# Products of zeros on TensorE in the planned gaps of a fused attention and MoE kernel, with a place for each in PSUM, and new planner constants

## The chip, the cores and the metric

One core of a Trainium2 chip runs the whole program. The metric is the device time of one execution in microseconds (us); of a kernel timed several times the median counts. TensorE (PE) multiplies, VectorE (DVE), ScalarE (ACT) and GpSimd (POOL) do the elementwise work, and the DMAs are issued from the queue of SyncE (SP), or early on from that of ACT. TensorE writes its results to PSUM, which has 8 banks of 512 float32 columns. TensorE's clock has two levels, 1.2 and 2.4 GHz; the profile shows which of them was granted as a share of the upper one (0.5 or 1.0, or something between for a stretch that holds both).

## The reference

Three stages follow one another, on 4 batches of 576 tokens:

```python
scores = scale * q @ k.T                       # 4 x 8 heads, 576 x 576, head size 64
scores = scores + cum[:, None] - cum[None, :]  # cum: running sum of log f
attn = softmax(causal(scores)) @ v             # (4, 8, 576, 64) -> x: (2304, 512)
y = (x @ w_a) * (x @ w_b) @ w_out              # 512 -> 1536 -> 512
h = y @ w_in                                   # 512 -> 1024
out = layernorm(h * softmax(h)) * g_ln @ w_out2
```

All inputs and outputs are float32. Every large product is computed from operands split in a high and a low part, as three products added up in PSUM.

## The kernel before

The kernel doesn't issue its instructions in a fixed order. It first describes all work as operations (`op`, from line 78), each with an engine or a choice of engines, a planned duration, a key (its rank among the operations that are ready) and the buffers that it reads and writes. `Sched.run` (line 118) then plans a time line: on each engine it takes the ready operation that can start first, by rank among equals, books its planned duration, and gives buffers and PSUM banks to it. The result is a list sorted by planned start, and the instructions are issued in that order, so each engine's queue runs in the planned order, whatever the real times are. A product with n columns is planned at n/2400 us and a little (`t_mm`, line 44), which is the rate at the upper clock level. All ranks come from the constants in `Y` (line 291).

The work of the first part, up to some 470 us, is attention, head by head, with the first MoE products mixed in. The first batch's eight heads come twice: first their first 256 tokens (kind `K0`), then the rest (`K1`); the other 24 heads come whole (`KF`). One head goes through: a transpose of q and k on TensorE (line 842); the split of both by ACT (lines 862, 873), DVE (865, 877) and POOL (851); products that find the largest score of each row (906, with a mask added by 910) and their row maxima on DVE (930); a transpose of the maxima (948) and a copy of them by ACT (952); the scores (980, 984, 988); the exponential and its split by ACT (1031, 1047) and DVE (1053); the weighing of v (1088); and the division by the sum (1110 to 1142). As soon as 256 tokens of all heads of a batch are there, `up_unit` (line 1202) multiplies them with blocks of w_a and w_b (line 1211), whose weights were loaded and split by `load_cols` (lines 652 to 699). Attention's sums live in the banks from `state["lo"]` up; `lo` is 1 at first (line 491) and rises to 2 once the up products have begun, which use the banks below it (`bank_unit`, line 499); it would rise to 3 for a stream of tokens numbered `L3` or higher (line 1206), and the numbers go from 0 to 5. An up unit holds two banks at once, and while it has 256 tokens only the lower 256 columns of each are used. After about 610 us only the last two stages run.

At the end of the function stands a filler: a product of the identity, taken as bf16 (`identb`), with 256 columns of `cmask` that hold only zeros, written to the upper half of bank 0 (lines 1725 and 1726). It is meant for gaps of TensorE's plan: from the time `at` on, for every planned TensorE operation that starts before `F1`, a gap over `FG` is filled to the share `FF` of its length with fillers of 0.109 us each. The time from which gaps are counted is

```python
at, todo = max(CONST.last[x].done for x in ("ident", "cmask")) + 0.2, []
```

and `CONST.last["cmask"]` is the operation described last that writes `cmask`. The mask itself is set at the start (the operation that calls `k_cmask`, lines 531 and 532). The load of the layer norm's weights, which lie in the mask's memory, names it as written too (lines 1386 and 1387), with the rank of the end of attention:

```python
op(("SP", 0.68), Z[-1], lat=2.0, fn=lambda: issue(
    out=gln, in_=moe2_g_ln.rearrange("(c p) -> p c", p=P)), w=[(CONST, "gln"), (CONST, "cmask")], nbytes=4e3)
```

Of the kernel before, what the change touches and what calls it, by code (L numbers as in the profile page):

```python
# [45 lines left out]


class Buf:
    __slots__ = ("cls", "slot", "left", "users", "last", "readers", "free", "cand", "pool", "lo", "skip", "at")

    def __init__(self, cls, cand=None, pool=None):
        self.cls, self.cand, self.pool = cls, cand, pool
        self.lo = 0
        self.skip = cls == "att"
        self.slot = None
        self.left = 0
        self.users = []
        self.last = {}
        self.readers = {}
        self.free = 0.0  # L60
        self.at = 0.0


class Op:
    __slots__ = ("n", "opts", "fn", "key", "deps", "after", "ready", "bufs", "done", "eng", "port", "lat", "nbytes", "start", "scheduled", "nwait", "dma", "lean")


class Sched:
# [21 lines left out]
    def op(self, opts, key, fn, r=(), w=(), after=(), lat=0.0, port=False, nbytes=0, lean="BIAS"):  # L90

        o = Op()
        o.n = len(self.ops)
        o.opts = [opts] if isinstance(opts, tuple) else list(opts)
        o.dma = o.opts[0][0] == "SP"
        o.lean = lean
        if o.dma and key < Y["D2"]:
            o.opts.append(("ACT", o.opts[0][1]))
        o.fn, o.key, o.lat, o.port, o.nbytes = fn, key, lat, port, nbytes
        deps = set(after)  # L100
        bufs = []
        for b, p in r:
            if p in b.last:
                deps.add(b.last[p])
            b.readers.setdefault(p, []).append(o)
            if b not in bufs:
                bufs.append(b)
        for b, p in w:
            if p in b.last:
                deps.add(b.last[p])  # L110
            for x in b.readers.get(p, ()):
                if x is not o:
                    deps.add(x)
            b.readers[p] = []
            b.last[p] = o
            if b not in bufs:
                bufs.append(b)
        deps.discard(o)
        for b in bufs:
            b.left += 1  # L120
            b.users.append(o)
        o.deps, o.bufs = deps, bufs
        o.after = []
        o.scheduled = False
        o.ready = 0.0
        self.ops.append(o)
        return o
# [163 lines left out]
Y = {  # L291
    "Z0": 13.6157,
    "T0": 4.814,
    "T1": 6.0827,
    "TA": 11.0028,
    "TF": 18.2246,
    "U0": 1.7014,
    "U1": 0.2661,
    "UF": 2.0658,
    "UL": 1.2999,  # L300
    "LEAD": (1.2959, 6.2184),
    "SHRINK": 1.9788,
    "W0": 39.7443,
    "WD0": 2.7456,
    "WN": 3,
    "WD1": 0.0,
    "WD2": 11.7263,
    "EZ": 8.5785,
    "EO": 17.1538,
    "TE": 28.5361,  # L310
    "DL": 0,
    "BIAS": 0.3046,
    "UO": (7.4065, 7.7687, 10.1476),
    "UD": 22.6745,
    "UK": 375.6785,
    "L3": 13,
    "TL": (0.0, 0.0),
    "F1": 262.9889,
    "FG": 0.1893,
    "FF": 0.7352,  # L320
    "RA": 1,
    "HM": 0,
    "HC": 2,
    "YC": 20.1189,
    "T2": 11.1014,
    "TB": 1,
    "HB": 1,
    "F2": 344.7825,
    "LATE": -0.6454,
# [28 lines left out]
def kernel(  # L358
# [14 lines left out]
    nc = tc.nc  # L373
    B, H, S, D = q.shape
    P = 128
    NP = H // 2
    BH = B * H
    NT, DM = out.shape
    KD = DM // P
    FF = moe_w_a.shape[1]  # L380
# [118 lines left out]
    def bank_unit(last, c):  # L499
        def cand(_):  # L500
            if last and c >= NF - Y["HB"]:
                return [(b, 1) for b in range(4, 8)]
            return [(b, 1) for b in range(8 if last else state["lo"])]
        return cand
# [10 lines left out]
    def k_set(s, part, eng=None):  # L515
        b = type("B", (), {"slot": s})
        if part < 2:
            cs = slice(0, 2 * P) if part == 0 else slice(2 * P, SP)
            eng.memset(SB(b).bitcast(F32)[D:, cs], -1.0)
            eng.memset(MB(b).bitcast(F32)[D:, cs], 0.0)  # L520
            eng.memset(MB(b).bitcast(F32)[D:D + 2, cs], 1.0)
            if part == 0:
                eng.memset(mts[:, s], 0.0)
                eng.memset(mts[:, s, 0:2], 1.0)
        else:
            nc.gpsimd.memset(SA(b).bitcast(F32)[:, S:SP], 0.0)
            nc.gpsimd.memset(SB(b).bitcast(F32)[:D, S:SP], 0.0)
            nc.gpsimd.memset(MB(b).bitcast(F32)[:D, S:SP], 0.0)
# [18 lines left out]
    for s in range(NSET):  # L547
        o = op([("POOL", 1.0), ("DVE", 1.0)], 20.0, None, w=[(CONST, f"pad{s}a")])
        o.fn = lambda s=s, o=o: k_set(s, 1, ENG[o.eng])
        op(("POOL", 0.6), 20.0, lambda s=s: k_set(s, 2), w=[(CONST, f"pad{s}")])  # L550
    PADS = [(CONST, "set0"), (CONST, "set1"), (CONST, "set2")]
    PADS2 = [(CONST, f"pad{s}{x}") for s in range(NSET) for x in ("", "a")]

# [647 lines left out]
    def up_unit(i, c, key, last):  # L1201
        b, q0, q1 = STR[i]
        n_ = q1 - q0
        u = [s_.buf("unit", bank_unit(last, c if i == NS - 1 else 0)) for _ in range(2)]
        u[0].lo = 3 if i >= Y["L3"] else 2
        uo = (0, n_) if len(u) == 1 else (0, 0)

        def mm(m, ks):
            for kk in ks:
                for n, (wp, xx) in enumerate(((0, 0), (1, 0), (0, 1))):  # L1210
                    nc.tensor.matmul(  # L1211
                        bank(u[m % len(u)], uo[m], n_), lhsT=wv(m, wp, c)[:, kk], rhs=xsv(i, xx, kk),
                        start=(kk == 0 and n == 0), stop=(kk == KD - 1 and n == 2))

        if c < Y["PK"] and i <= B:
            parts = [(m, (kk,)) for kk in range(KD) for m in range(2)]
        elif c == NF - 1 and i <= B:
            parts = [(m, (kk, kk + 1)) for kk in (0, 2) for m in range(2)]
        else:
            parts = [(m, range(KD)) for m in range(2)]  # L1220
        for j, (m, ks) in enumerate(parts):
            rx = [(xsb[i][p], (s, p)) for p in ks for s in "hl"]
            rw = [(WB[c], ((m, k_), s)) for k_ in ks for s in "hl"]
            op((PE, t_mm([n_] * 3 * len(ks))), key + Y["UK"] + 0.01 * j, lambda m=m, ks=ks: mm(m, ks),
               r=rx + rw, w=[(u[m % len(u)], m)])
        at = s_.buf("at")
        gt = s_.buf("gt")
        atv = lambda: ats[:, :n_]
        gtv = lambda: gts[:, gt.slot * XT:gt.slot * XT + n_]

        op(("ACT", t_act(n_, True)), key - 50.0, lambda: nc.scalar.copy(  # L1231
            out=atv(), in_=bank(u[0], 0, n_)), r=[(u[0], 0)], w=[(at, 0)])
        op(("DVE", t_dve(n_)), key - 50.0, lambda: nc.vector.tensor_tensor(  # L1233
            out=gtv(), in0=bank(u[-1], uo[1], n_), in1=atv(), op=ALU.mult),
           r=[(u[-1], 1), (at, 0)], w=[(gt, 0)])
        op(("SP", 0.44), key - 50.0, lat=1.45, fn=lambda: issue(out=gs[i][c], in_=gtv()),
           r=[(gt, 0)], w=[(GD, (i, c))], nbytes=512.0 * n_)
# [484 lines left out]
        fn(*a)  # L1722
    order = s_.run(state)

    def filler():
        nc.tensor.matmul(ps[:, 2 * P:512], lhsT=identb, rhs=cmask[:, :2 * P], start=True, stop=True)

    def fill(us):  # L1730
        return lambda: [filler() for _ in range(int(us / 0.109))]

    at, todo = max(CONST.last[x].done for x in ("ident", "cmask")) + 0.2, []
    for o in order:
        if o.eng == PE and o.start < Y["F1"]:
            gap = o.start - at
            if gap > Y["FG"]:
                todo.append((at, fill(gap * Y["FF"])))
            at = max(at, o.start + dict(o.opts)[PE])
    def emit(o):  # L1740
        now[:] = [o]
# [37 lines left out]
```

## Time and profile before

| | |
|---|---|
| median of 3 executions | 931.98 us (931.57 to 932.89) |
| the profiled execution | 932.68 us |
| its span, first to last instruction | 931.0 us |
| mean granted TensorE clock in the records | 0.983 |
| TensorE busy | 892.6 us, 96% of the span, 4926 products |
| DVE, ACT, POOL busy | 637.7, 474.9, 169.9 us (69, 51, 18%) |

Three ways of reading are used below. The windows view gives for any stretch the busy time of each engine and the granted clock. The list of a line's instructions gives the shortest, the median and the longest duration of each kind. The chain of waits follows the end of the program back to its start. A product's record in the timeline lasts longer than its turn on the engine, as the next one starts before it ends; the chain's pieces, or the distance of two starts, give the time that one takes from the engine.

### The profile page before, as it was taken

To read this page: it belongs to the slowest core of one execution; us is meant where nothing else is said; L and a number is where in the kernel's file an instruction comes from. 1 tells how busy PE (TensorE), PEld (TensorE's weight loads), DVE (VectorE), ACT (ScalarE), POOL (GpSimd) and SP (SyncE) were. 2 spreads that over 40 slices of the span, in tenths; PEclk is the share of its full clock that TensorE was granted. 3 is DMA by queue.
4 is the path that set the end of the run, shared out by engine and by line. 5 is a ranking of instruction groups with operands and counts; after the bars stand their busy time and mean duration, and the time that the engine had idled before them with its cause. 6 is when DMAs were issued, how large, how long until landed. Compare 5 with 4: busy or idle time off the path is not lost.

```text
span 931.0 us, 14134 instructions
## 1 busy us (share of the span) xinstructions
PE 892.6 (96%) x4926; PEld 775.5 (83%) x4926; DVE 637.7 (69%) x1238; ACT 474.9 (51%) x892; POOL 169.9 (18%) x297
## 2 busy tenths in 40 slices
PE   5878989999999999999999999999999999999996
PEld 3768978999888888888888898988888888888884
DVE  6768897777765457665476255789687777767784
ACT  3776785766664546555565143555333434243342
POOL 5556665232231103111111000000000000000000
PEclk9978998999999999999999999999999999999999
DMA  6244654433433323322266233353211111111101
GB/s 149 66 118 129 182 157 107 100 89 88 96 81 81 83 76 87 98 68 62 68 227 209 98 123 109 114 165 106 69 46 46 46 46 45 46 40 42 33 23 35
DMA packets 109947, 85.00 MB, mean 91 GB/s; under 512 B 69778, under 2 KB 91412, under 8 KB 109876
## 3 DMA queue, kind: packets, MB, share of 16 engines
q1 hardware_dynamic: 105508, 81.78, 30.9%
q10 hardware_dynamic: 4368, 2.32, 1.0%
q8 instruction: 39, 0.64, 0.3%
q14 instruction: 32, 0.26, 0.1%
HBM read 57.38 MB, written 19.55 MB: 83 GB/s over the span
## 4 chain that ended last, share of the span: by engine, by line
PE 91%; DVE 3%; ACT 3%; DMA 1%; issue 1%; POOL 0%; ACTq 0%; DVEq 0%; SPq 0%
PE ps L1211 31%; PE ps L1493 16%; PE ps L1686 11%; PE ps L1088 10%; PE ps L1579 9%; PE ps L988 3%; PE ps L906 3%; PE ps L980 3%; PE ps L842 2%; PE ps L1671 2%; DVE mts L930 1%; PE ps L948 1%; DMA nat<-in_q_dram 1%; PE ps L910 0%; DVE sets L865 0%
## 5 line engine op out<-in xcount | busy, mean ns | idle before, releaser
L1211 PE MATMUL ps<-xs,wt 128*128 128x256 f32 (+1 forms) x1728 | 331.7, 344 | 1.0 <-ACT xs L1178 0.3
L1211 PEld LDWEIGHTS ps<-xs,wt 128*128 128x128 f32 x1728 | 271.6, 193 | 34.4 <-POOL xs L1183 0.5
L1088 PE MATMUL ps<-pexp,VS 128*128 128x64 f32 (+5 forms) x600 | 104.6, 322 | 5.5 <-DVE sets L865 4.4
L1088 PEld LDWEIGHTS ps<-pexp,VS 128*128 128x128 f32 x600 | 96.5, 205 | 10.8 <-DVE sets L865 4.5
L1493 PE MATMUL ps<-wt,sets 128*128 128x512 f32 (+1 forms) x420 | 91.8, 370 | 0.0
L1493 PEld LDWEIGHTS ps<-wt,sets 128*128 128x128 f32 x420 | 72.9, 189 | 12.8
L1686 PE MATMUL ps<-wt 128*128 128x512 f32 x324 | 80.4, 393 | 1.8 <-DVE wt L1677 1.0
L1233 DVE TENSOR_TENSOR fw<-ps,fw 128x256 f32<-128x256 f32 (+1 forms) x72 | 40.0, 555 | 59.1 <-PE ps L1211 37.9
L1579 PE MATMUL ps<-wt,xs 128*128 128x512 f32 x306 | 79.3, 392 | 0.0
L1231 ACT COPY fw<-ps 128x256 f32<-128x256 f32 (+1 forms) x72 | 34.6, 481 | 79.5 <-PE ps L1211 70.3
L1053 DVE TENSOR_TENSOR pexp<-fw,pexp 128x768 fp32r<-128x768 f32 (+1 forms) x45 | 45.6, 1014 | 42.5 <-ACT pexp L1047 42.0
L1686 PEld LDWEIGHTS ps<-wt 128*128 128x128 f32 x324 | 59.9, 188 | 15.1 <-DVE wt L1677 1.9
L1481 ACT CAST wt<-nat 128x512 fp32r<-128x512 f32 (+1 forms) x60 | 34.6, 580 | 69.0 <-PE ps L1493 64.7
L1040 POOL TENSOR_SCALAR_AFFINE_SELECT fw<-fw 128x128 f32<-128x128 f32 (+1 forms) x120 | 36.4, 332 | 169.4 <-ACT fw L1031 169.3
L1579 PEld LDWEIGHTS ps<-wt,xs 128*128 128x128 f32 x306 | 56.5, 188 | 11.2
L933 DVE CUSTOM_DVE_ANT_0 ps<-ps,cmask 128x512 f32<-128x512 f32 (+4 forms) x100 | 53.8, 553 | 15.2 <-PE ps L906 12.9
L1485 DVE TENSOR_TENSOR wt<-nat,wt 128x512 fp32r<-128x512 f32 (+1 forms) x60 | 38.0, 635 | 28.6 <-ACT wt L1481 27.3
L980 PE MATMUL ps<-sets 128*128 128x320 f32 (+4 forms) x200 | 52.5, 310 | 2.8 <-ACT fw L1031 0.9
L988 PE MATMUL ps<-sets 67*128 67x288 f32 (+6 forms) x200 | 53.5, 342 | 0.2
L906 PE MATMUL ps<-sets 66*128 66x512 f32 (+2 forms) x192 | 48.5, 350 | 3.5 <-DVE sets L877 1.8
L1031 ACT ACTIVATE fw<-ps 128x768 f32<-128x768 f32 (+1 forms) x48 | 39.5, 836 | 23.2 <-PE ps L988 22.5
L1047 ACT CAST pexp<-fw 128x768 fp32r<-128x768 f32 (+1 forms) x48 | 41.2, 859 | 9.8 <-POOL fw L1040 9.4
(173 smaller groups left out, 1464.0 us busy)
## 6 DMA issues: line engine op xcount, KB each, us to landing
gs<-fw SPq DMA_DIRECT2D x36, 256.0 KB
nat<-gs SPq DMA_DIRECT2D x36, 256.0 KB
fw<-in_moe_w_out_dram SPq DMA_DIRECT2D x15, 512.0 KB
sets<-sets SPq DMA_DIRECT2D x48, 144.0 KB
fw<-in_moe_w_b_dram SPq DMA_DIRECT2D x10, 512.0 KB
fw<-in_moe_w_a_dram SPq DMA_DIRECT2D x9, 512.0 KB
nat<-gs SPq DMA_DIRECT2D x36, 128.0 KB
nat<-in_k_dram SPq DMA_DIRECT2D x33, 128.0 KB
```

Of the source, the lines that this page charges most:

```text
L906: nc.tensor.matmul(bank(ms[part], o, w), lhsT=MB(st)[:D + 2, i * P:(i + 1) * P], rhs=SB(st)[:D + 2, k0:k0 + w], start=True, stop=not pm)
L933: nc.vector.tensor_tensor_reduce(out=x, in0=x, in1=cmask[:n, off:off + w], scale=1.0, scalar=-3.0e38, op0=ALU.add, op1=ALU.max, accum_out= ...
L980: nc.tensor.matmul(dst, lhsT=SA(st)[:, ks], rhs=MA(st)[:, q0:q1], start=True, stop=False)
L988: nc.tensor.matmul(dst, lhsT=SB(st)[:depth, ks], rhs=MB(st)[:depth, q0:q1], start=False, stop=True)
L1047: op(("ACT", t_act(n, K.pm)), key + K.rk[5] + 6.8 + 0.9 * i, lambda bh=bh, n=n, pf=pf: nc.scalar.copy(out=pexp[:, 64 * bh.slot:64 * bh.slo ...
L1053: o.fn = lambda o=o, bh=bh, bl=bl, n=n, pf=pf: ENG[o.eng].tensor_tensor(out=pexp[:, 64 * bl.slot:64 * bl.slot + n], in0=pf(), in1=pexp[:, ...
L1088: nc.tensor.matmul(bank(u, K.uo + q0, q1 - q0), lhsT=V[:, vp], rhs=src[:, o:o + q1 - q0], start=(k_ in K.first and ip == 0), stop=(k_ in K ...
L1211: nc.tensor.matmul(bank(u[m % len(u)], uo[m], n_), lhsT=wv(m, wp, c)[:, kk], rhs=xsv(i, xx, kk), start=(kk == 0 and n == 0), stop=(kk == K ...
L1233: op(("DVE", t_dve(n_)), key - 50.0, lambda: nc.vector.tensor_tensor(out=gtv(), in0=bank(u[-1], uo[1], n_), in1=atv(), op=ALU.mult), r=[(u ...
L1493: nc.tensor.matmul(bank(py, 512 * d, n), lhsT=WO[c][0][:, wp * DM:(wp + 1) * DM][:, ds_], rhs=ghv(gb, gp)[:, :n], start=(c == 0 and i == 0 ...
L1579: nc.tensor.matmul(bank(bk, 0, 512), lhsT=yc(yx, yp)[:, kk], rhs=wi(wx, wp, kk), start=(n == 0), stop=(n == 5))
L1686: nc.tensor.matmul(bank(po, 0, DM), lhsT=zp[:, c], rhs=w2(c, wp), start=(c == 0 and i == 0), stop=(c == NF2 - 1 and i == 2))
```

## The change

The filler products get their own place. The operation that first writes the mask is kept in `MASKS`, where it is described, and `at` is taken from that. `place(at)` looks at the planned use of the banks at a gap's start: if an up unit of 256 tokens is in the middle of its sum (`half`), the filler goes to the spare upper half of that unit's bank and neither starts nor ends a sum; else it goes to the free bank whose next use is farthest off, with a start and an end of its own; if no bank is free, the gap stays. `FG` falls from 0.1893 to 0, `FF` goes from 0.7352 to 0.7329, `F1` from 262.99 to 268.18. Some forty other constants of `Y` change, most of them ranks, so the planned order changes.

```diff
     "T1": 6.0827,          ->  5.9693
     "U0": 1.7014,          ->  2.802
     "U1": 0.2661,          ->  1.3074
     "WD2": 11.7263,        ->  11.4893
     "UD": 22.6745,         ->  19.9599
     "F1": 262.9889,        ->  268.1794
     "FG": 0.1893,          ->  0.0
     "FF": 0.7352,          ->  0.7329
     "HB": 1,               ->  0
     "EL": -2.8131,         ->  2.403
...
+    MASKS = [CONST.last["ident"], CONST.last["cmask"]]
     PADS = [(CONST, "set0"), (CONST, "set1"), (CONST, "set2")]
...
         u = [s_.buf("unit", bank_unit(last, c if i == NS - 1 else 0)) for _ in range(2)]
+        for x in u:
+            x.half = len(u) == 2 and n_ == 2 * P
...
-    def filler():
-        nc.tensor.matmul(ps[:, 2 * P:512], lhsT=identb, rhs=cmask[:, :2 * P], start=True, stop=True)
-    def fill(us):
-        return lambda: [filler() for _ in range(int(us / 0.109))]
-    at, todo = max(CONST.last[x].done for x in ("ident", "cmask")) + 0.2, []
+    held = [(b, min(o.start for o in b.users), max(o.done for o in b.users),
+             [o.start for o in b.users if o.eng == PE])
+            for q in s_.queue.values() for b in q if b.pool == "bank" and b.users]
+    def place(at):
+        next_ = [1.0e9] * 8
+        for b, t0, t1, mm in held:
+            if b.half and min(mm) < at <= max(mm):
+                return b.slot, False
+            for x in range(b.slot, b.slot + b.free):
+                if t1 >= at:
+                    next_[x] = min(next_[x], 0.0 if t0 <= at else t0)
+        x = max(range(8), key=lambda x: next_[x])
+        return (x, True) if next_[x] > 0.0 else None
+    def fill(us, x, alone):
+        def go():
+            for _ in range(int(us / 0.109)):
+                nc.tensor.matmul(ps[:, 512 * x + 2 * P:512 * x + 512], lhsT=identb, rhs=cmask[:, :2 * P],
+                                 start=alone, stop=alone)
+        return go
+    at, todo = max(o.done for o in MASKS) + 0.2, []
     for o in order:
         if o.eng == PE and o.start < Y["F1"]:
             gap = o.start - at
-            if gap > Y["FG"]:
-                todo.append((at, fill(gap * Y["FF"])))
+            if gap > Y["FG"] and place(at):
+                todo.append((at, fill(gap * Y["FF"], *place(at))))
             at = max(at, o.start + dict(o.opts)[PE])
```

## Rows read from the trace of the kernel before

**Rows 1.** The page: TensorE's busy time, and the granted clock in 40 slices.

```profile
PE 892.6 (96%) x4926; PEld 775.5 (83%) x4926; DVE 637.7 (69%) x1238; ACT 474.9 (51%) x892; POOL 169.9 (18%) x297
...
PEclk9978998999999999999999999999999999999999
```

**Rows 2.** Windows: stretch; its length, PE, PEld, DVE, ACT, POOL busy; granted clock, DMA.

```profile
13.00:52.00 39.00, 33.71 (x153) 28.97 (x154) 24.73 (x55) 25.14 (x62) 21.50 (x33) 1.00 0.38 104
52.00:83.20 31.20, 21.87 (x117) 18.54 (x115) 24.42 (x35) 21.07 (x43) 17.70 (x17) 0.73 0.43 122
55.90:59.40 3.50, 2.92 (x14) 2.66 (x15) 3.50 (x6) 2.35 (x5) 0.95 (x1) 0.52 0.33 91
63.00:73.00 10.00, 7.33 (x32) 6.56 (x33) 7.68 (x11) 7.36 (x17) 6.53 (x6) 0.50 0.29 78
79.90:83.20 3.30, 3.30 (x17) 2.81 (x15) 2.26 (x4) 0.75 (x2) 2.63 (x3) 0.50 0.53 167
83.20:130.00 46.80, 46.39 (x370) 44.18 (x369) 40.32 (x61) 37.42 (x74) 28.39 (x27) 1.00 0.62 174
130.00:151.30 21.30, 15.93 (x86) 13.37 (x85) 15.75 (x28) 12.47 (x27) 13.18 (x20) 0.76 0.47 116
137.90:144.30 6.40, 5.86 (x26) 5.56 (x27) 3.76 (x7) 2.82 (x5) 4.42 (x7) 0.50 0.71 164
148.00:151.30 3.30, 3.30 (x16) 2.99 (x15) 2.03 (x4) 2.19 (x5) 0.70 (x2) 0.50 0.73 188
151.30:253.90 102.60, 100.88 (x754) 96.11 (x753) 77.95 (x155) 66.75 (x113) 31.76 (x65) 1.00 0.37 90
253.90:257.20 3.30, 3.30 (x14) 2.73 (x13) 2.17 (x3) 3.05 (x5) 1.86 (x4) 0.50 0.66 144
258.00:610.00 352.00, 352.00 (x1916) 307.44 (x1915) 204.00 (x381) 177.24 (x292) 43.89 (x99) 1.00 0.36 107
610.00:931.00 321.00, 313.15 (x1513) 261.06 (x1511) 237.42 (x499) 126.77 (x273) 1.56 (x2) 1.00 0.18 55
```

**Rows 3.** Weight loads of line 910 in four stretches: shortest, median, longest ns; starts.

```profile
L910 PEld LDWEIGHTS <-ident x16: 146/146/146, 13.7 to 49.8; 128*128 128x128 bf16 x16
...
L910 PEld LDWEIGHTS <-ident x5: 98/98/99, 52.7 to 54.7; 128*128 128x128 bf16 x5
...
L910 PEld LDWEIGHTS <-ident x1: 146/146/146, 81.3 to 81.3; 128*128 128x128 bf16 x1
...
L910 PEld LDWEIGHTS <-ident x8: 98/98/99, 92.3 to 116.7; 128*128 128x128 bf16 x8
```

**Rows 4.** The chain of waits: two runs of line 1211's 256-column products (start, us).

```profile
50.16 2.03 PE ps L1211 x9
...
89.32 2.96 PE ps L1211 x24
```

**Rows 5.** Groups of TensorE up to 270 us: the bf16 products at their widest.

```profile
L910 PE MATMUL ps<-cmask,ident 128*128 128x128 bf16 x48 | 12.7, 269 | 0.0
...
L984 PE MATMUL ps<-ident,cmask 128*128 128x128 bf16 x32 | 9.1, 284 | 0.0
```

**Rows 6.** Timelines of POOL and TensorE: the mask, and the first product of scores.

```profile
3.30 0.29 POOL L532 TENSOR_SCALAR_AFFINE_SELECT cmask<-cmask 128x128 bf16<-128x128 bf16 x1
...
13.38 0.55 PE L906 MATMUL ps<-sets 66*128 66x256 f32 x1 [0.43 <-issue]
```

**Rows 7.** The last products on TensorE, with the idle time before them.

```profile
910.36 1.10 PE L1671 MATMUL ps<-ident,xrw 128*128 128x128 f32 x8 [1.25 <-DVE xrw L1637]
...
925.76 0.39 PE L1686 MATMUL ps<-xs,wt 128*128 128x512 f32 x1
```

**Rows 8.** TensorE's waits up to 270 us: total us, times, longest.

```profile
PE ps L948 <- DVE mts L930: 8.9, 8, 1.9
...
PE ps L1211 <- ACT fw L1231: 0.2, 1, 0.2
```

More of the change, by code (lines that the diff above doesn't have):

```diff
@@ L48 @@
 class Buf:
-    __slots__ = ("cls", "slot", "left", "users", "last", "readers", "free", "cand", "pool", "lo", "skip", "at")
+    __slots__ = ("cls", "slot", "left", "users", "last", "readers", "free", "cand", "pool", "lo", "skip", "at", "half")
     def __init__(self, cls, cand=None, pool=None):
-        self.cls, self.cand, self.pool = cls, cand, pool
+        self.cls, self.cand, self.pool, self.half = cls, cand, pool, False
         self.lo = 0
@@ L293 @@
     "T0": 4.814,
-    "T1": 6.0827,
+    "T1": 5.9693,
     "TA": 11.0028,
     "TF": 18.2246,
[L297 to L302, printed above, removed]
+    "U0": 2.802,
+    "U1": 1.3074,
+    "UF": 2.0785,
+    "UL": 1.1356,
+    "LEAD": (1.2959, 6.0955),
+    "SHRINK": 1.795,
     "W0": 39.7443,
@@ L306 @@
     "WD1": 0.0,
-    "WD2": 11.7263,
+    "WD2": 11.4893,
     "EZ": 8.5785,
-    "EO": 17.1538,
+    "EO": 17.3183,
     "TE": 28.5361,
@@ L313 @@
     "UO": (7.4065, 7.7687, 10.1476),
-    "UD": 22.6745,
+    "UD": 19.9599,
     "UK": 375.6785,
-    "L3": 13,
+    "L3": 15,
     "TL": (0.0, 0.0),
-    "F1": 262.9889,
-    "FG": 0.1893,
-    "FF": 0.7352,
+    "F1": 268.1794,
+    "FG": 0.0,
+    "FF": 0.7329,
     "RA": 1,
@@ L323 @@
     "HC": 2,
-    "YC": 20.1189,
+    "YC": 21.644,
     "T2": 11.1014,
     "TB": 1,
-    "HB": 1,
+    "HB": 0,
     "F2": 344.7825,
     "LATE": -0.6454,
[1 row of a table removed]
[1 row of a table added]
     "BA": -0.177,
```

16 rows, old and new, of the table Y are left out of this document.

## The prediction

> **What bounds the kernel now.** I read the page first: TensorE is busy for 96% of the span, and its granted clock dips only in the first 260 us [rows 1]. The windows view, cut where the clock changes, then splits the kernel in two [rows 2]. From 151 us on TensorE is all but full: 1.7 us idle up to 253.9, none from 258 to 610, and 7.9 us after 610, of which 4.9 lie behind its last product (925.76 + 0.39 = 926.15, to 931.0) [rows 2, 7]. What comes earlier there ends the program earlier, and what TensorE does twice makes it later. Before 151 us it has slack: idle 5.3 us in stage A (13 to 52), 9.3 in stage B (52 to 83.2), 5.4 in stage C (130 to 151.3), and only 0.4 in the stretch between B and C.
>
> Six stretches stand at a granted clock of 0.50 to 0.52 (one of them, D, at 253.9): 3.5, 10.0, 3.3, 6.4, 3.3 and 3.3 us [rows 2]. The seventh is hidden. The records give stage A a clock of 1.00, but a weight load of line 910 takes 146 ns there 16 times of 16, from 13.7 to 49.8 us, just as at 81.3, where 0.50 is recorded, and 98 ns from 52.7 on and wherever else 1.00 is recorded [rows 2, 3]. So by the durations all of stage A ran at 1.2 GHz, with TensorE 86% busy. A 256-column product takes 2.03/9 = 0.226 us at the lower level and 2.96/24 = 0.123 at the upper [rows 4], so 45% of TensorE's time at the lower level would go. Busy time there: 33.71 in A, 2.92 + 7.33 + 3.30 = 13.55 in B, 5.86 + 3.30 = 9.16 in C, 3.30 in D; at 45%: 15.3, 6.2, 4.2 and 1.5, in all 27.2 us. That is the ceiling of what the clock alone can return.
>
> **The fillers.** The change adds them; it doesn't move them. The widest bf16 products in the first 270 us have 128 columns and belong to lines 910 and 984 [rows 5]; a filler has 256, and none is there. The code says why: the gaps were counted from the last writer of the mask, which is the load at the end of attention, beyond F1. Now they are counted from the real mask, ready at 3.59 us [rows 6].
>
> How much zero work is that? The planner books products at the upper clock, so its gaps are idle time plus what the lower clock costs. Busy from 13 to 258 is 222.9 us (33.71, 21.87, 46.39, 15.93, 100.88, 3.30, and 0.8 to 258, full) [rows 2], 196 at the upper clock. If that stretch falls from 245 to some 230 us, 34 us of gap stand there, and about 5 before 13 us. At 0.733, that is 29 us of zeros, some 265 fillers at the booked 0.109 us, 0.123 by the nearest row [rows 4], and a quarter of each gap stays as margin.
>
> **What the clock returns**, if the fillers hold it up. In a stage where TensorE has room, the next engine takes over, and I price it by the shares that DVE and ACT reach in the nearest stretch with a full clock and a full TensorE, 83.2 to 130: DVE 40.32/46.8 = 0.86, ACT 37.42/46.8 = 0.80 [rows 2].
> A: TensorE needs 33.71 - 15.3 = 18.4, DVE 24.73/0.86 = 28.8, ACT 25.14/0.80 = 31.4. ACT is late next: 39.0 becomes 31.4, so -7.6. Ends: 0 and -15.3.
> B: DVE 24.42/0.86 = 28.4, ACT 26.3; 31.2 becomes 28.4, so -2.8. Ends: 0 and -6.2.
> C: DVE 15.75/0.86 = 18.3; 21.3 becomes 18.3, so -3.0. Ends: 0 and -4.2.
> D: TensorE is full through and behind it, so all of it counts: -1.5.
> Together -14.9, all of it kept, since TensorE has no slack behind it.
>
> **What the fillers cost.** TensorE works in order, so a filler that is still running when its successor is ready delays it and all behind it. At the upper clock the quarter of margin covers that. At the lower it does not: 0.733 x 0.226/0.109 = 1.52 of the gap. This must happen until the clock first rises. Up to 13.38 us the first scores wait for the decay sums, not for TensorE [rows 6], which hides most of it. I take one more lapse of the shortest length seen, 3.3 us, at 0.52 each: +1.7. Ends: 0, and the 29 us if every filler stood in the way; the low end is nearer, as TensorE's idle in A, B and C (20 us) shows real gaps at real places.
>
> **The rest.** The new ranks reorder a TensorE that is full from 151 us on, so they can win there no more than its idle, 1.7 us, and the last pair's wait of 1.25 [rows 2, 7]; EL puts one pair's closing products elsewhere in just that tail. They could also lose as much. I take 0 between -3 and +3. HB lets the last up unit use any bank, where TensorE is full: 0, between the same ends. L3 rises from 13 to 15 and is compared with numbers up to 5: 0. The marks and `place` run before launch: 0.
>
> Sum: -14.9 + 1.7 = -13.2. The profiled execution took 932.68, so 919.5; the median stands 0.7 below it, so **918.8 us**.
>
> **A rule of the notes.** The Trainium skill, in "TensorE: Matmul & The Clock Gate", Part 1, says that the low clock is the resting state and that sustained activity releases it; by that alone a TensorE that is 86% busy for 39 us would not have stayed low. The rows disagree: 146 ns throughout. The same page warns in its caveats on clock events that the recorded ones have been seen to be unreliable, which fits the 1.00 beside 146 ns. By the first rule term A would go, and the sum would be that of rival 1.
>
> **The rivals.**
> 1. Stage A gains nothing: it was not slow by its clock, as the recorded 1.00 says, but by its waits. Then B, C and D give -7.3, less 1.7: -5.6, which is 926.4 by the median. For it: the record, and 5.3 us of idle. Against: 146 ns, and the clock was up at 52.7 us, right behind nine dense 256-column products that end at 52.2 [rows 3, 4]; a filler has as many columns. Chance 0.12.
> 2. The fillers wait. Each goes to a bank that is free by the plan; where the bank's last reader is late, TensorE stands still and all behind it too. The waits of line 948 for DVE cost 8.9/8 = 1.1 us each, that of line 1211 for its bank's reader 0.2 [rows 8]. Twelve waits of 1.1 eat the whole gain: 932. The Trainium skill's "PSUM — Partial Sum Buffer", section on bank collisions, asks for that order, since two engines must not touch one bank at a time; no run here shows it yet. Against: the bank with the farthest next use has often long been idle. Chance 0.05.
> 3. Nothing is emitted after all (no bank is found, or gaps are shorter than one filler), and only the ranks act: 932, within 3. Against: attention leaves bank 0 alone at first. Chance 0.03.
> 4. Slower: the clock stays low in stage A with the fillers in place. Its planned gap is 31.4 - 18.4 = 13.0 us, the zeros 9.5 booked and 9.5 x 0.226/0.109 = 19.7 real; TensorE then needs 33.7 + 19.7 = 53.4 where the stage took 39.0: +14.4, so some 946. It decides from the share of the stage that runs low: warm the sum is 18.4 + 9.5 = 27.9, cold 53.4, and 39.0 is reached at (39.0 - 27.9)/(53.4 - 27.9) = 44%. For it: 39 us at 86% busy did not raise the clock. Against, as in rival 1: dense products did. Chance 0.08.
>
> **The numbers.** The forecast case has 0.72. Its ends: -27.2 with the idle of A to C also shrinking (down to about 900), and a few us short of nothing. The range of 902 to 930 holds it but for 0.05, and rival 1; rivals 2 to 4 lie outside. No change means within 0.2%, 1.9 us, about what a measurement of this kernel can tell. Faster: 0.72 + 0.12 + a little of rivals 2 and 3, 0.86. Same: 0.05. Slower: 0.08 and 0.01 of rival 3, 0.09.
>
> **What would show it.** Right: some 265 bf16 products of 256 columns before 268 us; weight loads of line 910 at 98 ns from about 13 us on; the six low stretches gone; ACT and DVE at 0.80 or more in the first 50 us; line 1211's first full run before 80 us instead of 89; from there the same sequence, 13 us earlier, to the end. Wrong: 146 ns beside fillers (rival 4), waits of TensorE put down to a filler's bank (rival 2), or ACT and DVE no denser while TensorE idles between zeros (rival 1, or a chain of latencies that I priced too low).

## The result, and the profile after

The changed kernel takes 917.05 us (median of 4 executions, 916.50 to 921.45), the kernel before, run beside it, 932.43: a ratio of 0.9846, with a 95% interval of 0.9813 to 0.9878. The profiled execution took 916.50 us, its span 914.8, so 16.2 us less than the span of before; by the medians the gain is 15.4 us. The forecast was 918.8, its range 902 to 930.

The page of the kernel after, its lines of TensorE's busy time and of the granted clock in 40 slices:

```profile
PE 897.6 (98%) x5241; PEld 780.7 (85%) x5241; DVE 637.0 (70%) x1240; ACT 472.0 (52%) x886; POOL 170.3 (19%) x301
...
PEclk9999999999999999999999999999999999999999
```

There are 5241 - 4926 = 315 more products than in [rows 1], and no slice shows a low clock any more. What they are stands in the list of one line's instructions after; line 1747 is the new filler, line 911 the old line 910:

```profile
L1747 PEld LDWEIGHTS <-ident x315: 97/98/151, 1.4 to 255.5; 128*128 128x128 bf16 x158
L1747 PE MATMUL ps<-cmask,ident x315: 269/273/421, 3.3 to 255.5; 128*128 128x256 bf16 x158
...
L911 PEld LDWEIGHTS <-ident x21: 97/98/101, 13.6 to 45.8; 128*128 128x128 bf16 x21
```

All 315 are fillers, and line 911's weight loads take 97 to 101 ns from the first one at 13.6 us on, where [rows 3] had 146: by the durations the first stage now runs at 2.4 GHz. The windows of the kernel after, cut at the same work as [rows 2] where the order allows it (columns as there):

```profile
13.00:42.74 29.74, 28.05 (x243) 24.16 (x242) 25.60 (x53) 23.77 (x59) 19.41 (x29) 1.00 0.47 128
42.74:74.00 31.26, 28.82 (x233) 24.75 (x231) 27.16 (x41) 25.81 (x51) 22.40 (x25) 1.00 0.51 141
74.00:150.00 76.00, 74.47 (x604) 68.57 (x603) 63.65 (x109) 53.93 (x110) 45.86 (x55) 1.00 0.54 151
150.00:254.00 104.00, 103.83 (x755) 98.50 (x754) 74.06 (x148) 67.94 (x109) 31.56 (x65) 1.00 0.38 92
258.00:594.00 336.00, 336.00 (x1827) 293.26 (x1827) 195.07 (x361) 167.26 (x274) 38.90 (x94) 1.00 0.36 108
```

To see where the 16.2 us came from, two marks serve that stand in both orders: the eighth transpose of row maxima, which ends stage A, and the last up product. In the timelines, before and then after:

```profile
51.99 0.61 PE L948 MATMUL ps<-ident,mts 128*1 128x128 f32 x2
```

```profile
42.74 0.38 PE L949 MATMUL ps<-ident,mts 128*1 128x128 f32 x2
```

And in the list of the up products, first before, then after (the last number ahead of the forms is the last start):

```profile
L1211 PE MATMUL ps<-xs,wt x1728: 277/389/775, 43.6 to 605.8; 128*128 128x256 f32 x96, 128*128 128x512 f32 x96
```

```profile
L1214 PE MATMUL ps<-xs,wt x1728: 277/387/496, 36.3 to 589.5; 128*128 128x256 f32 x96, 128*128 128x512 f32 x96
```

Stage A gave 51.99 - 42.74 = 9.25 us. From there to the last up product it was 553.8 us and is 546.8: another 7.0. Behind that the same time passes: 931.0 - 605.8 = 325.2 before, 914.8 - 589.5 = 325.3 after. Among the waits of TensorE after (us in total, times, longest), up to 280 us:

```profile
PE ps L1747 <- POOL cmask L531: 3.3, 1, 3.3
PE ps L1089 <- DVE sets L866: 1.9, 1, 1.9
...
PE ps L949 <- DVE mts L931: 0.8, 3, 0.4
```

The waits for DVE's row maxima shrank from 8.9 us [rows 8] to 0.8: zeros stand in most of that time now. No filler waits for a reader of its bank: TensorE's only wait at line 1747 is that for the mask; the fillers' weight loads wait 1.4 us for the identity, and 2.3 us in three gaps for which the profile names no releaser.

### The profile page after: what moved, and what is told of

The parts are those of the page before. It is cut to its first block, busy times and chain, and to the rows that moved or that the text cites. A ratio compares the mean times of both kernels' runs of the same rounds, so it can differ in the third digit from the quotient of the medians.

```text
span 914.8 us, 14766 instructions
## 1 busy us (share of the span) xinstructions
PE 897.6 (98%) x5241; PEld 780.7 (85%) x5241; DVE 637.0 (70%) x1240; ACT 472.0 (52%) x886; POOL 170.3 (19%) x301
## 4 chain that ended last, share of the span: by engine, by line
PE 92%; DVE 3%; ACT 2%; issue 1%; DMA 0%; POOL 0%; ACTq 0%; DVEq 0%; POOLq 0%
PE ps L1214 32%; PE ps L1496 16%; PE ps L1689 11%; PE ps L1582 9%; PE ps L1089 8%; PE ps L989 3%; PE ps L907 3%; PE ps L981 3%; PE ps L843 2%; PE ps L1747 2%; PE ps L1674 2%; DVE sets L866 1%; DVE mts L931 0%; PE ps L949 0%; DMA nat<-in_k_dram 0%
## 5 line engine op out<-in xcount | busy, mean ns | idle before, releaser
L1214 PE MATMUL ps<-xs,wt 128*128 128x256 f32 (+1 forms) x1728 | 327.1, 340 | 0.0
L1214 PEld LDWEIGHTS ps<-xs,wt 128*128 128x128 f32 x1728 | 267.3, 189 | 32.9 <-ACT fw L1234 0.2
L1089 PE MATMUL ps<-pexp,VS 128*128 128x64 f32 (+5 forms) x600 | 97.8, 306 | 2.8 <-DVE sets L866 1.9
L1089 PEld LDWEIGHTS ps<-pexp,VS 128*128 128x128 f32 x600 | 89.3, 190 | 8.1 <-DVE sets L866 2.2
L1054 DVE TENSOR_TENSOR pexp<-fw,pexp 128x832 fp32r<-128x832 f32 (+1 forms) x47 | 47.0, 1001 | 42.5 <-ACT pexp L1048 42.0
L1041 POOL TENSOR_SCALAR_AFFINE_SELECT fw<-fw 128x128 f32<-128x128 f32 (+1 forms) x120 | 34.2, 314 | 162.0 <-ACT fw L1032 162.0
L1747 PE MATMUL ps<-cmask,ident 128*128 128x256 bf16 x315 | 45.9, 281 | 3.3 <-POOL cmask L531 3.3
L981 PE MATMUL ps<-sets 128*128 128x320 f32 (+4 forms) x200 | 48.6, 291 | 0.4 <-ACT sets L953 0.2
L989 PE MATMUL ps<-sets 67*128 67x288 f32 (+6 forms) x200 | 48.8, 321 | 0.0
L907 PE MATMUL ps<-sets 66*128 66x512 f32 (+3 forms) x192 | 44.7, 328 | 1.7 <-DVE sets L866 0.6
```

What stands on the lines that cost most here:

```text
L907: nc.tensor.matmul(bank(ms[part], o, w), lhsT=MB(st)[:D + 2, i * P:(i + 1) * P], rhs=SB(st)[:D + 2, k0:k0 + w], start=True, stop=not pm)
L981: nc.tensor.matmul(dst, lhsT=SA(st)[:, ks], rhs=MA(st)[:, q0:q1], start=True, stop=False)
L989: nc.tensor.matmul(dst, lhsT=SB(st)[:depth, ks], rhs=MB(st)[:depth, q0:q1], start=False, stop=True)
L1054: o.fn = lambda o=o, bh=bh, bl=bl, n=n, pf=pf: ENG[o.eng].tensor_tensor(out=pexp[:, 64 * bl.slot:64 * bl.slot + n], in0=pf(), in1=pexp[:, ...
L1089: nc.tensor.matmul(bank(u, K.uo + q0, q1 - q0), lhsT=V[:, vp], rhs=src[:, o:o + q1 - q0], start=(k_ in K.first and ip == 0), stop=(k_ in K ...
L1214: nc.tensor.matmul(bank(u[m % len(u)], uo[m], n_), lhsT=wv(m, wp, c)[:, kk], rhs=xsv(i, xx, kk), start=(kk == 0 and n == 0), stop=(kk == K ...
```

## The experiments

Two theories were set against each other at first. The clock theory is the forecast's: the fillers hold the clock, and that is the gain. The order theory gives it to the new ranks. All runs below were timed beside the kernel before, whose median was 932.39 (runs 1 to 4), 931.24 (5 to 8), 932.66 (9 to 11) and 931.52 (12).

### 1 and 2: the ranks alone, the fillers alone

Run 1 keeps the new constants and issues no filler; run 2 keeps the fillers and takes all other constants from the kernel before.

```diff
-        if o.eng == PE and o.start < Y["F1"]:
+        if o.eng == PE and o.start < 0.0:
```

```diff
-    "T1": 5.9693,
+    "T1": 6.0827,
...
-    "EL": 2.403,
+    "EL": -2.8131,
```

> The changed kernel with its new constants and no products of zeros at all. Clock theory: the gain comes from the fillers, so this is as slow as the kernel before, 932 within 3 us, with line 911's weight loads at 146 ns from 13 to about 52 us and TensorE's low stretches back. Order theory: the new ranks give a good part of the gain, so 926 or less.

> The changed kernel's code with the ranks of the kernel before (only F1, FG and FF are the new ones). Clock theory: the fillers alone give the gain, 917 to 921 us. Order theory: 925 or more.

Measured: run 1 took 927.39 us, a ratio of 0.995 (0.9929 to 0.9971); run 2 took 918.84, 0.9843 (0.9814 to 0.9871). So the fillers alone bring nearly everything, 13.6 us, and the order theory falls as the main cause. But the ranks alone bring 5.0, which the clock theory had not expected, and which is less than the order theory said. The two don't add up: together they gave 15.4.

Run 2's profiled execution, 919.82 us, lost 2.6 us in a place that has nothing to do with attention. Its span is 918.1 us and its last up product starts at 590.3:

```profile
L1214 PE MATMUL ps<-xs,wt x1728: 276/387/501, 36.5 to 590.3; 128*128 128x256 f32 x96, 128*128 128x512 f32 x96
```

Behind that 327.8 us pass, where before and after have 325.2 and 325.3: near 900 us, long behind the last filler, the clock fell. The windows of run 2 there, and the same 16 products in the timelines of run 2 and of the kernel after:

```profile
898.20:901.60 3.40, 3.40 (x8) 2.73 (x9) 3.09 (x9) 0.17 (x1) 0.00 (x0) 0.50 0.00 0
```

```profile
898.14 6.48 PE L1689 MATMUL ps<-wt 128*128 128x512 f32 x16 [0.88 <-DVE wt L1680]
```

```profile
897.41 3.93 PE L1689 MATMUL ps<-wt 128*128 128x512 f32 x16 [1.01 <-DVE wt L1680]
```

Run 10's profiled execution lost the same there (327.9 us). So a part of the 1.8 us between run 2 and the change can be this lapse and not the order of work.

The list of up products and the windows of run 1 show what the ranks do:

```profile
L1214 PE MATMUL ps<-xs,wt x1728: 274/389/562, 43.6 to 599.7; 128*128 128x256 f32 x96, 128*128 128x512 f32 x96
```

```profile
13.00:52.00 39.00, 33.74 (x153) 29.01 (x154) 24.79 (x54) 25.25 (x62) 21.52 (x33) 1.00 0.38 103
...
62.50:72.70 10.20, 8.47 (x37) 7.68 (x38) 7.71 (x12) 7.50 (x16) 7.05 (x6) 0.51 0.31 79
130.20:133.50 3.30, 3.30 (x18) 2.97 (x18) 3.20 (x7) 2.47 (x7) 3.18 (x3) 0.55 0.00 2
```

Stage A is that of before to about a tenth, and its end stands at 51.97 us. Behind it the last up product comes after 547.7 us, not 553.8. The new order has two low stretches there, 13.5 us in all; the old one had six, 29.8 us [rows 2]. That the 6.1 us come from the shorter low stretches fits, but no run separates it from the order itself.

### 3 and 4: fillers at the start only, fillers in stage A only

```diff
-    "F1": 268.1794,
+    "F1": 13.0,        # run 3; 43.0 in run 4
```

> The changed kernel with fillers only before planned operations that start before 13 us. They raise the clock, then nothing fills the gaps. If a raised clock holds by the real work alone, line 911's weight loads stay at 98 ns through the first stage and the time is 917 to 922. If it must be held by fillers, the loads go back to 146 ns within some us of 13 and the time is 928 to 932.

> The changed kernel with fillers only before planned operations that start before 43 us, the end of the first stage (A). Clock theory: stage A keeps its gain of 9.3 us (the eighth transpose of row maxima at 42.7 us), and the later low stretches come back and cost what they cost before, some 5 to 7 us: 921 to 924. If the later stretches cost nothing, 917.

Run 3 took 925.42 us (ratio 0.9918, 0.9893 to 0.9944), run 4 926.16 (0.9921, 0.9893 to 0.9949). Against run 1's 927.39 neither is clearly faster. Run 4 lies 2 us above what was expected. In run 3, whose last filler starts at 14.6 us, the windows show a clock that rises and isn't held; beside them line 911's weight loads in the same two stretches:

```profile
13.00:19.40 6.40, 4.23 (x33) 2.91 (x31) 3.99 (x11) 2.68 (x7) 1.90 (x4) 0.98 0.88 232
19.40:43.00 23.60, 21.96 (x105) 19.45 (x105) 16.09 (x35) 16.78 (x42) 13.74 (x22) 0.50 0.21 61
```

```profile
L911 PEld LDWEIGHTS <-ident x4: 98/98/101, 13.8 to 17.1; 128*128 128x128 bf16 x4
...
L911 PEld LDWEIGHTS <-ident x10: 145/146/146, 21.9 to 36.6; 128*128 128x128 bf16 x10
```

The second half of run 3's expectation holds, that fillers must go on; the time was a few us lower than it said, since it was set against 932 and not against the ranks' 927. This run also closes the gap in the records: with a fall to record, the profile gives 0.50 to the very stretch that it called 1.00 in the kernel before, at the same 146 ns.

Run 4 is the surprise. Its eighth transpose comes at 42.60 us, so stage A is won in full, and yet the last up product is no earlier than in run 1:

```profile
L1214 PE MATMUL ps<-xs,wt x1728: 274/389/562, 36.2 to 599.3; 128*128 128x256 f32 x96, 128*128 128x512 f32 x96
```

Its windows show where the 9.4 us went:

```profile
47.10:50.90 3.80, 3.75 (x21) 3.40 (x21) 2.59 (x5) 2.56 (x6) 2.03 (x2) 0.58 0.49 150
54.50:64.80 10.30, 8.40 (x36) 7.62 (x37) 7.78 (x13) 7.50 (x16) 6.96 (x6) 0.50 0.28 62
68.50:75.00 6.50, 6.01 (x27) 5.46 (x27) 4.50 (x8) 3.08 (x7) 4.06 (x5) 0.50 0.18 57
102.40:105.80 3.40, 3.40 (x17) 3.31 (x16) 3.01 (x6) 1.32 (x3) 1.90 (x2) 0.51 0.49 159
126.40:132.90 6.50, 5.62 (x25) 4.89 (x26) 5.28 (x9) 4.38 (x11) 4.64 (x5) 0.50 0.04 15
```

Five low stretches with 27.18 us of TensorE's work, where run 1 has two with 11.8. At 45% of that [rows 4] they cost up to 12.2 us; the way from stage A's end to the last up product is 556.7 us, 9.9 more than with the whole change. All of it is lost where these stretches lie: at the sixteenth transpose of row maxima run 4 is already 10.3 us behind the kernel after, having been 0.14 ahead at the eighth. In the timelines of run 4 and of the kernel after:

```profile
141.57 0.49 PE L949 MATMUL ps<-ident,mts 128*1 128x128 f32 x3
```

```profile
131.25 0.49 PE L949 MATMUL ps<-ident,mts 128*1 128x128 f32 x3
```

### 9: fillers behind stage A only

```diff
-            if gap > Y["FG"] and place(at):
+            if at > 43.0 and gap > Y["FG"] and place(at):
```

> The changed kernel with fillers only in gaps that begin after 43 us of the plan, the counterpart of the run that had them only before. Stage A then runs at the lower clock (line 911's weight loads at 146 ns, the eighth transpose of row maxima near 52 us). If a stage's gain is kept wherever the later clock is held, A's 9.2 us are lost to the end: 925 to 927. If A's lateness is taken up again later, because other engines use the time to work ahead, 920 to 923. If it gives no more than the new ranks without fillers: 927.

It took 924.61 us (0.9926, 0.9902 to 0.9949); the profiled execution, 927.25, lies 2.6 us above that median (the five: 924.37 to 928.14), at a mean granted clock of 0.999. Behind stage A its clock is up:

```profile
52.00:155.00 103.00, 97.32 (x782) 87.82 (x781) 86.18 (x138) 73.79 (x148) 63.27 (x71) 1.00 0.52 148
```

The eighth transpose comes at 51.79, the last up product is

```profile
L1214 PE MATMUL ps<-xs,wt x1728: 277/387/562, 43.4 to 600.2; 128*128 128x256 f32 x96, 128*128 128x512 f32 x96
```

so 548.4 us lie between, and the 9.05 us by which it trails the changed kernel at the end of A have become 10.7. In this execution A's lateness isn't taken up again. The median lies between the first two cases: it trails the change's by 7.6 us, which would leave room for 1.5 us taken up again, and what the other executions did no profile shows. Set side by side (the first two columns and the last from the profiled execution, `time` the median):

| | end of A | from there to the last up product | time | profiled execution |
|---|---|---|---|---|
| before | 51.99 | 553.8 | 932.4 | 932.68 |
| ranks alone (run 1) | 51.97 | 547.7 | 927.4 | 926.70 |
| fillers in A alone (run 4) | 42.60 | 556.7 | 926.2 | 926.25 |
| fillers behind A alone (run 9) | 51.79 | 548.4 | 924.6 | 927.25 |
| old ranks, all fillers (run 2) | 42.89 | 547.4 | 918.8 | 919.82 |
| the change | 42.74 | 546.8 | 917.1 | 916.50 |

Against run 1, A's fillers alone win 1.2 us by the medians, those behind A 2.8, neither clear of the spread; both together win 10.3. So each half needs the other. Fillers in A bring its end forward by 9.4 us, which was lost again in run 4, where the clock then fell; and fillers behind a late A found little to save, as in the profiled executions the low stretch at 62.5 us of run 1 cost nothing. That shows in the timelines of run 1 and run 9, at the twelfth transpose of row maxima:

```profile
92.84 0.49 PE L949 MATMUL ps<-ident,mts 128*1 128x128 f32 x3
```

```profile
92.66 0.49 PE L949 MATMUL ps<-ident,mts 128*1 128x128 f32 x3
```

From the eighth, both need 40.87 us, the one with 10 us of low clock, the other with none. So in these two executions something other than TensorE's clock sets that way; in both, TensorE waits there for DVE's line 866, 4.4 us in run 1, 1.9 us behind zeros in run 9. Which engine it is was not tried.

### 5 to 8: more and fewer zeros

```diff
-    "FF": 0.7329,
+    "FF": 0.35,        # run 5; 0.55, 0.9 and 1.0 in runs 6 to 8
```

> The changed kernel with FF 0.35 in place of 0.7329: about half the zeros. If the clock needs most of the gaps filled, low stretches come back (line 911's weight loads at 146 ns somewhere in the first 50 us, a granted clock of 0.5 in some stretch) and the time is 921 to 927. If any filling holds it, 917 as with the change, or up to 1 us faster since less stands in the way.

> The changed kernel with FF 0.55. If the clock needs most of the gaps filled, some low stretches and 918 to 923; if not, 917 as with the change.

> The changed kernel with FF 0.9. Fillers in the way: only a tenth of each planned gap is left as margin; if the fillers that stand in the way are what limits the gain, 918 to 921. If the planned gaps are real, 916 to 918, with no low stretch.

> The changed kernel with FF 1.0, no margin. Fillers in the way: some 10 us more zeros than with the change; if a third of that is on the path, 919 to 922. If the planned gaps are real, 916 to 918.

| FF | fillers | time | ratio (95%) | low stretches in the profile |
|---|---|---|---|---|
| 0.35 | 131 | 918.92 | 0.9871 (0.9825 to 0.9918) | 53.5 to 60.5, 71.5 to 73.5 |
| 0.55 | 227 | 917.50 | 0.9852 (0.9810 to 0.9893) | about 3 us at 56 |
| 0.7329 (the change) | 315 | 917.05 | 0.9846 (0.9813 to 0.9878) | none |
| 0.9 | 388 | 921.88 | 0.9896 (0.9858 to 0.9934) | none |
| 1.0 | 432 | 921.61 | 0.9899 (0.9872 to 0.9926) | none |

Between 0.35 and 0.73 the times can't be told apart. Too many zeros do cost: with FF 0.9, 73 more fillers put the time up by 4.8 us, though the mean granted clock of its executions is 0.998 to 1.000. The intervals of 0.9 and of the change just touch, but of the 13 executions with 0.9 and 1.0 none took less than 920.46 us, and of the four with 0.55, timed beside them, none more than 918.64. Whether half the zeros (918.92) are better than 0.9, these runs can't tell. The eighth transpose shows the same in A: 42.45 us at 0.35, 42.74 with the change, 43.85 at 0.9, 44.89 at 1.0. Runs 5 and 6 went below what was expected, as a low stretch of some us did little harm; runs 7 and 8 came out on the side of fillers in the way, run 7 a touch above.

### 10: only the long gaps; 12: dense zeros in the middle only

```diff
-    "FG": 0.0,
-    "FF": 0.7329,
+    "FG": 0.6,
+    "FF": 0.6,
```

> The changed kernel with FG 0.6 and FF 0.6: fillers only in planned gaps over 0.6 us, to 60% of them. If the clock needs only the long gaps filled, 915 to 918 and no low stretch, with fewer zeros in the way; if the short gaps count as well, low stretches come back between 45 and 75 us and it takes 918 to 921.

It took 918.26 us (0.9841, 0.9810 to 0.9872) with 221 fillers; the profiled execution has one low stretch, 54 to 58 us. The two expectations meet here, and the run decides nothing but that short gaps, together with a smaller share, matter little to the time.

```diff
-                todo.append((at, fill(gap * Y["FF"], *place(at))))
+                todo.append((at, fill(gap * (Y["FF"] if 40.0 < at < 85.0 else 0.35), *place(at))))
```

> The changed kernel with FF 0.35 in gaps that begin before 40 or after 85 us of the plan and 0.7329 between, where the run with 0.35 throughout had its low stretches (53 to 61 and 71 to 74 us). That run was 0.3 us ahead of the change at the eighth transpose of row maxima, fell 3.8 behind by the twelfth, and won back 1.5 to the end of the up products. If both gains add up and the middle holds the clock: 1 to 2 us under the change, 915 to 916.5. If the middle falls low again, as what comes before it is thinner: 917 to 919.

A miss: 922.44 us (0.9894, 0.9864 to 0.9925). The middle fell low although its fillers are those of the change, and a further low stretch came at 126; in the windows of run 12:

```profile
54.00:58.00 4.00, 3.94 (x21) 3.62 (x22) 2.04 (x4) 3.88 (x10) 1.84 (x3) 0.59 0.16 37
71.00:76.00 5.00, 4.27 (x22) 3.96 (x23) 2.22 (x5) 1.98 (x5) 2.59 (x4) 0.66 0.50 145
126.00:130.00 4.00, 4.00 (x21) 3.48 (x21) 3.45 (x7) 2.88 (x8) 3.51 (x3) 0.57 0.00 0
```

So here the small gains of thinner zeros did not add to the hold of dense ones. No run beat the change, and none of these was tried further.

### 11: the bank

```diff
-        x = max(range(8), key=lambda x: next_[x])
+        x = min((x for x in range(8) if next_[x] > 0.0), key=lambda x: next_[x], default=0)
```

> The changed kernel with a filler's bank chosen as the free one whose next use comes soonest, not last. Place theory (my rival 2): fillers then wait for late readers of their bank, or products wait behind them, 920 or more, with waits of line 1747 for DVE or ACT in the list. Else 917 as with the change.

It took 917.49 us (0.9843, 0.9813 to 0.9872), and on TensorE its fillers wait for nothing but the mask. Among banks that the plan holds free, the choice is worth nothing that shows. A late reader of a filler's bank turns up only in runs 7 and 10, once each: 0.2 us for ACT's line 1234. Writing all fillers to bank 0, as the old code meant to, was not tried, and what the place in an open sum's spare half is worth stays open too.

## Why the prediction was right, point by point

**The bound.** Right. The first stage ran at the lower clock and the records did not say so; run 3 shows the same durations under a recorded 0.50. What was gained ahead of the last up product reached the end: the 325 us behind it are the same to 0.1 before and after, and to 0.2 in every run but 2 and 10, with their low stretch near 900 us.

**The old fillers were never issued.** Right: 315 products of line 1747 now, none before. The count was to be 265; 315 x 0.109/0.7329 makes at least 46.8 us of planned gap, where the forecast had 39. Their price was booked well: 18 zeros of the kernel after take from 36.73 to 38.62 us, 0.105 each, and the first five, by their duration at the lower clock, 0.204. The timeline also shows when the clock rose: the 14 zeros from 7.56 us on take 0.163 each on average, the nine from 10.06 on 0.109:

```profile
3.28 1.22 PE L1747 MATMUL ps<-cmask,ident 128*128 128x256 bf16 x5 [3.28 <-POOL cmask L531]
4.30 0.42 PE L843 MATMUL ps<-ident,nat 128*128 128x128 f32 x1
...
7.56 2.45 PE L1747 MATMUL ps<-cmask,ident 128*128 128x256 bf16 x14
9.84 0.38 PE L843 MATMUL ps<-ident,fw 128*128 128x128 f32 x2
10.06 1.15 PE L1747 MATMUL ps<-cmask,ident 128*128 128x256 bf16 x9
11.04 0.38 PE L843 MATMUL ps<-ident,fw 128*128 128x128 f32 x2
...
36.73 2.14 PE L1747 MATMUL ps<-cmask,ident 128*128 128x256 bf16 x18
38.62 0.49 PE L1089 MATMUL ps<-pexp,VS 128*128 128x256 f32 x2
```

**Term A**, -7.6: measured -9.25. The shares were met to the digit, DVE at 25.60/29.74 = 0.86 and ACT at 23.77/29.74 = 0.80. What was off is ACT's work: the forecast took all 25.14 us that ACT did before the mark as needed for it, and 23.77 were enough. The new order isn't the reason: run 2, whose queues have the order of before, reached the mark at 42.89 us with 59 instructions of ACT in that window (23.55 us) where before had 62, so three had only been done early. The window of run 2:

```profile
13.00:42.89 29.89, 28.13 (x245) 24.37 (x244) 25.80 (x54) 23.55 (x59) 19.94 (x30) 1.00 0.48 128
```

That ACT is the engine that sets the stage is not shown: by the same shares DVE's 25.60 us, which were to be 24.73, need 29.8 us and ACT's 23.77 need 29.7, and both fit the measured 29.74.

**Terms B, C and D**, -7.3, and the fillers' cost, +1.7: together -5.6 for what lies behind A, measured -7.0 (with the old ranks, run 2: 553.8 - 547.4 = 6.4). The sum is near, the picture behind it is not, so that nearness is in part luck. The forecast gave each stage a term of its own and called all of it kept. Runs 4 and 9 show that they hang together: A's gain survives only where the later clock is held, and the later clock is worth 9.9 us behind an early A (run 4 against the change) and nothing that the profiles show behind a late one (run 1 against run 9). The fillers' cost is real but not where it was put: at the start nothing was lost (first scores at 13.36 us, 13.38 before; the row names no releaser [rows 6], but the same time with TensorE faster and full of zeros agrees that TensorE did not set it), while FF 0.9 shows what a thinner margin costs, 4.8 us.

**The ranks**, 0 within 3: wrong in its step, though not in the sum. They bring 5.0 us by themselves. The step looked for idle time behind 151 us and left out what an order can win before: run 1 has 13.5 us of low clock where before had 29.8, which fits, though it isn't shown by itself: between runs 1 and 9 a low stretch cost nothing. With fillers the ranks matter little: 918.84 with the old, 917.05 with the new, a difference that these runs can't tell from none. EL, HB and L3 did nothing that shows behind the last up product, as run 1's 925.0 - 599.7 = 325.3 us there are those of before.

**The rule of the notes.** The Trainium skill, "TensorE: Matmul & The Clock Gate", Part 1, has sustained activity release the low clock. Run 3 bears out the forecast's choice not to lean on that with the profile's busy time as the measure: at 21.96/23.60 = 93% busy by the windows, TensorE stayed at 0.50 for 23.6 us. In the kernel after, the clock rose in a run of 14 zeros from 7.56 us on; what the work lacked, these runs don't show.

**The rivals.** Rival 1 falls with 98 ns in stage A and the 9.25 us it gained. Rival 2 falls: no filler of the change waits for a bank's reader, and run 11, made to provoke that, is as fast. Rival 3 falls with 315 fillers. Rival 4 needed 44% of stage A at the lower clock; it had none.

## What to carry to other kernels

Read the clock from the duration of one instruction that recurs, not from the clock's record alone: here a stage that was slow from the start was recorded as 1.00. Zeros in TensorE's real gaps held the clock here where the work didn't, but they had to go on through every stage with gaps, since the 9.4 us won early in run 4 were lost again in the next low stretches; and they should leave a margin, as a quarter too many cost 4.8 us, while with a quarter to over half fewer no loss is clear of the spread. Test a stage's worth with the others both held and not held, because such gains need not add up.

## What the runs showed of the hardware

A clock that was up at 13 us had fallen by 19.4 in run 3, whose last zero starts at 14.6; TensorE was busy for 4.23 of those 6.40 us. It did not come back in the next 23.6 us, at 93% busy. A low stretch came back again and again behind the same wait for DVE near 54 to 62 us (runs 1, 4, 5, 6, 10, 12; TensorE waits there 4.4 us in run 1 and 1.9 in run 12), also in run 12, which has the change's fillers around it. The clock can also fall near 900 us, where no zeros are (runs 2 and 10, 2.6 us each). Executions of one kernel differ accordingly: six of run 12 range from 918.61 us at a mean granted clock of 0.998 to 927.37 at 0.988, and the slowest of the changed kernel, 921.45, had 0.994 where the fastest, 916.50, had 0.999. That is about one us for each 0.001 of mean clock in these two. It is no rule for all: run 9's executions of 924.37 and 927.25 us had 0.997 and 0.999.
